# Two chunks of one batch taken out of the casting load: fp32 load, a fold on GpSimd and VectorE, and a quadrant first stage

## The chip, the cores and the metric

The kernel runs on one core of a Trainium2 chip. The metric is the device time of one execution in microseconds. It is told as a median over runs, and a profiled execution has a time of its own beside the span of its trace.

## The reference

Two layers follow each other. The first filters x (8 batches, 3072 rows, 256 columns) along the rows in the frequency domain: `irfft(rfft(x) * (filt_r + i filt_i))`, column by column. The second takes the result as 24576 tokens of 256 and computes `max(h @ w1, h @ w2) @ w_out`, with 1024 hidden columns. Input and output are fp32.

## The kernel before

The row index of a batch is split as p * 32 + m, with 96 values of p and 32 of m. The filter is then a chain of small stages: a transform over p (first stage), a transform over m with the filter's product (second), the way back (third and fourth). The feed-forward layer works on 64 tiles of 384 tokens, eight to a batch. It is written as max(a, b) = max(a - b, 0) + b, so one hidden product with Wd = w1 - w2 (`moe_h`, L656, evicted as a relu), and an output product with Wo and M = w2 w_out (`moe_o`, L718 and L720).

All instruction streams are written out by hand. The main loop (L989 to L1018) goes through 64 steps for each batch. A step issues one `moe_h`, then what `mid` holds for it, then three to eight matmuls of `moe_o` for the tile before, and last what `plan` has put at that step. `now` and `later(n, ...)` put a call n steps on. So the stages of batch b + 1 are strewn between the tiles of batch b, and each engine takes its instructions strictly in the order in which they were issued. In `plan(0, 10, ...)` the first number is the batch, the second the step.

Until the main loop, batch 0 is brought through all its stages at once. Batch 1 has its own first stage, and all later batches another:

- **Batch 1** is loaded by `load_x` (L120) on GpSimd's DMA queue, which casts fp32 to bf16 on the way; one call takes two of the batch's eight chunks (chunk c holds m = 4c to 4c + 3). The calls for chunks 2 and 3, then `load_wo` (Wo), then a `prep_wd`, then the calls for chunks 4 and 5 and for 6 and 7 follow each other there (L880 to L884), and GpSimd's further `prep_wd` and `cast_w2` come behind them. `f1` (L359) does the first stage for two values of m: one matmul of the 96-column table C1 with 96 x 512 of x, evicted by ScalarE (even c) or VectorE (odd c) into `at`; after every second one SyncE stores the result to a scratch tensor `ad` in DRAM. `f1(1, 0)` to `f1(1, 3)` stand ahead of the loop, `f1(1, 4)` to `f1(1, 15)` at steps 5 to 12, and `f1_read` (L376) at step 13 reads it back transposed into `bt`, in three DMAs.
- **Batches 2 to 7** are loaded by `load_xf` (L127) in fp32, on SyncE's DMA queue, into one of three buffers XF[(8b + c) % 3], as two halves of 48 partitions each (g = 0, 1). In the first use of each buffer two more DMAs of 16 partitions (L134) fill the rows between. `fold` (L137) on GpSimd makes sum and difference of the two halves of p (L140, L141), in bf16. `s1` (L383) then needs only half-size transforms, which stand on quadrants of TensorE: for batch 2 four matmuls 64 x 64 x 512 (L397), for the others eight with 32 columns (L403). ScalarE evicts both of its PSUM tiles (L407), and `s1_store` writes them to `ad`.

In batch 0's steps, `plan_f2` puts `load_xf(2, c)` at steps 8, 8, 10, 12, 17, 20, 24, 28 and `fold(2, c)` at 10, 13, 16, 20, 24, 27, 30, 33. `visit` (L578) at step 25 is the first that reads batch 1's `bt` (`s2`, L435). PSUM has six banks for all of these tiles, in rotation, and two for the output.

SyncE's DMAs share eight semaphores in turn: in the built program each of its DMAs waits for the completion of the one eight places before it, besides waiting for its data.

The lines of the prediction: L125 is the issue of `load_x`, L130 and L134 of `load_xf`, L330 of Wo, L374 of `f1`'s store, L380 of `f1_read`, L341 and L348 are `prep_t` and `prep_m` (they build M), L366 is `f1`'s matmul and L369 its eviction on VectorE, L629 and L635 belong to `s4` (fourth stage), L793 to `t2`, L441 and L518 are products with the filter on VectorE, L281 is table arithmetic at the start.

Of the kernel before, what the change touches and what calls it, by code (L numbers as in the profile page):

```python
# [27 lines left out]
def kernel(  # L28
# [98 lines left out]
    def load_xf(b, c):  # L127
        src = x[b].rearrange("(h p m) d -> p h m d", h=2, m=NM)
        for g in range(2):
            nc.sync.dma_start(out=XF[(8 * b + c) % 3][64 * g:64 * g + 48],  # L130
                              in_=src[:, :, 4 * c + 2 * g:4 * c + 2 * g + 2, :])
            if b == 2 and c < 3:

                nc.sync.dma_start(out=XF[(8 * b + c) % 3][64 * g + 48:64 * g + 64],  # L134
                                  in_=src[0:16, :, 4 * c + 2 * g:4 * c + 2 * g + 2, :])

    def fold(b, c):  # L137
        t_ = x_tile(b, c).rearrange("p (s m) d -> p s m d", s=2)
        f = XF[(8 * b + c) % 3]
        G.tensor_tensor(t_[:, 0], f[:, 0], f[:, 1], OP.add)  # L140
        G.tensor_tensor(t_[:, 1], f[:, 0], f[:, 1], OP.subtract)  # L141
        xb[b, c] = t_
# [240 lines left out]
    def s1(b, c):  # L383
# [10 lines left out]
        bk.run(0.22)  # L394
        if b == 2:
            for g, r in ((0, 0), (1, 1), (0, 1), (1, 0)):
# [8 lines left out]
        for g in range(2):  # L405
            m0 = 4 * (c % 2) + 2 * g
            S.activation(at[:, m0:m0 + 2], pa[g], AF.Copy)  # L407
            bk.evict("S", 0.48, ks[g])
        if c % 2 == 1:
            later(52 - now[0][1] if c == 7 and b == 3 else 2 if c == 7 and b == 2 else 5 if c == 5 and b == 2 else 3, s1_store, b, c, at)  # L410

    def s1_store(b, c, at):
        for r in range(2):
            nc.sync.dma_start(out=ad[b][48 * r:48 * r + 48, 4 * c - 4:4 * c + 4], in_=at[64 * r:64 * r + 48])

# [466 lines left out]
    prep_wd(0, G)  # L882
    for c in (4, 6):
        load_x(1, c, 2)  # L884
    for q in range(1, 4):
# [13 lines left out]
    t2(0, (V, S))  # L899
    f1(1, 1, V)  # L900
    spin(1, I128, U[:, 0:8].rearrange("p u c -> p (u c)"))
    s4(0)
# [146 lines left out]
```

## Time and profile before

| What | us |
| --- | --- |
| median of 3 runs | 490.0 (489.99 to 490.71) |
| the profiled execution, its own time | 489.1 |
| span of its trace | 487.3 |
| PE (matmul) busy | 475.9, 98% of the span |
| DVE (VectorE) busy | 362.4, 74% |
| ACT (ScalarE) busy | 307.4, 63% |
| POOL (GpSimd) busy | 296.0, 61% |

The 1.8 us between the execution's own time and its span lie around the trace. A busy share is a mean over stages with different limits, and matmuls are pipelined, so the chain of work that ended last says more than the share. In that chain each piece has its start, its length, its engine and its line; where a piece of the same kind is longer at one place than at another, the engine lost time there. The timeline has for each row the start, the length, and in brackets the idle time ahead of it with what ended it. "SPq" is SyncE's DMA queue: a row tells when the issue began, not when the data landed.

### The profile page before, as it was taken

The numbers are of one execution on the slowest core, as the hardware profiler recorded it, in microseconds if no ns is written. First come the engines' busy times: TensorE is split into PE (matmuls) and PEld (weight loads), VectorE is DVE, ScalarE is ACT, GpSimd is POOL, SyncE is SP. The second block draws the span as 40 slices with busy tenths as digits, with TensorE's granted clock in tenths as the row PEclk, the third lists the DMA queues.
The fourth block names the chain that finished last, engine by engine and source line by source line (L and its number), as shares of the span: only waits on it lengthen the run. The fifth ranks groups of instructions, "written<-read, shape, count | busy, mean of one in ns | idle before, by whom it ended". The sixth has DMA issues, their size and how long they took to land.

```text
span 487.3 us, 15411 instructions
## 1 busy us (share of the span) xinstructions
PE 475.9 (98%) x6204; PEld 342.3 (70%) x6207; DVE 362.4 (74%) x589; ACT 307.4 (63%) x645; POOL 296.0 (61%) x378
## 2 busy tenths in 40 slices
PE   8689999999999999999999999999999999999996
PEld 4457777776677676776677676776777776777775
DVE  7886789987876878677786778777885878775542
ACT  5877488667764778468764677467774556354442
POOL 8695868559980698739874698738951266111110
PEclk9979999999999999999999999999999999999999
DMA  8999999898766889789876897789556523541112
GB/s 124 172 247 228 263 255 270 272 254 241 216 180 193 214 270 282 222 237 265 234 187 199 237 261 222 221 245 248 169 165 213 175 88 107 174 156 66 66 66 86
DMA packets 87816, 97.37 MB, mean 200 GB/s; under 512 B 9281, under 2 KB 67938, under 8 KB 87650
## 3 DMA queue, kind: packets, MB, share of 16 engines
q1 hardware_dynamic: 79010, 79.30, 57.7%
q0 software_dynamic: 8592, 17.01, 13.8%
q8 instruction: 48, 0.79, 0.7%
q14 instruction: 22, 0.18, 0.1%
q10 hardware_dynamic: 144, 0.09, 0.1%
HBM read 53.87 MB, written 47.19 MB: 207 GB/s over the span
## 4 chain that ended last, share of the span: by engine, by line
PE 93%; DVE 2%; DMA 2%; POOL 1%; issue 1%; ACT 0%; DVEq 0%; POOLq 0%
PE po L720 36%; PE ph L656 34%; PE po L718 9%; PE pc L612 3%; PE pa L403 2%; PE pz L547 2%; PE px L493 2%; DMA xb<-in_x_dram 2%; DVE pq L441 1%; DVE F L164 1%; PE pr L793 1%; POOL xb L125 1%; PE pz L459 1%; PE pa L366 1%; PE py L629 1%
## 5 line engine op out<-in xcount | busy, mean ns | idle before, releaser
L720 PE MATMUL po<-Wo,gt 128*128 128x256 bf16 x1528 | 263.1, 273 | 0.0
L661 ACT ACTIVATE gt<-ph 128x384 bf16<-128x384 f32 x347 | 165.9, 502 | 141.6 <-PE ph L656 136.8
L720 PEld LDWEIGHTS <-gt 128*128 128x128 bf16 x1528 | 144.2, 98 | 66.4 <-issue 12.4
L658 DVE TENSOR_SCALAR gt<-ph 128x384 bf16<-128x384 f32 x165 | 90.6, 552 | 46.2 <-PE ph L656 44.5
L656 PEld LDWEIGHTS <-Wd 128*128 128x128 bf16 x1024 | 99.0, 98 | 14.1 <-DVE pf L507 0.7
L668 POOL DMA_DIRECT2D out_dram<-ot x86 | 48.8, 568 | 98.1 <-DVE ot L731 87.8
L140 POOL TENSOR_TENSOR xb<-XF 128x512 bf16<-128x512 f32 x48 | 61.1, 1274 | 51.3 <-DMA XF<-in_x_dram 44.4
L503 DVE TENSOR_TENSOR pf<-px,F 128x1024 f32<-128x1024 f32 x60 | 71.1, 1218 | 18.7 <-PE px L493 7.0
L731 DVE TENSOR_SCALAR ot<-po 128x512 f32<-128x512 f32 x83 | 57.0, 686 | 18.8 <-PE po L720 18.2
L141 POOL TENSOR_TENSOR xb<-XF 128x512 bf16<-128x512 f32 x48 | 61.0, 1272 | 0.0
L407 ACT ACTIVATE at<-pa 128x512 bf16<-128x512 f32 x96 | 50.0, 603 | 4.0 <-PE pa L403 3.1
L533 POOL TENSOR_TENSOR ri<-pf 128x256 bf16<-128x256 f32 x60 | 43.8, 730 | 14.3 <-DVE pf L503 14.1
L534 POOL TENSOR_TENSOR ri<-pf 128x256 bf16<-128x256 f32 x60 | 43.6, 727 | 0.0
L556 ACT ACTIVATE zt<-pz 128x512 bf16<-128x512 f32 x60 | 31.3, 600 | 9.2 <-PE pz L547 9.2
L617 ACT ACTIVATE ce<-pc 128x384 f32<-128x384 f32 x56 | 23.7, 490 | 3.5 <-PE pc L612 2.1
L441 DVE TENSOR_TENSOR pq<-px,F 128x1024 bf16<-128x1024 f32 x19 | 22.1, 1219 | 2.6 <-PE px L435 2.3
L403 PE MATMUL pa<-xb,CT 64*32 64x512 bf16 x320 | 16.2, 381 | 0.0
L612 PEld LDWEIGHTS <-zr 48*128 48x128 bf16 x896 | 12.6, 93 | 4.4 <-issue 3.6
L612 PE MATMUL pc<-G,zr 48*128 48x48 bf16 x896 | 14.8, 180 | 0.0
L493 PE MATMUL px<-bt,U 64*32 64x256 bf16 x432 | 14.4, 272 | 0.0
L514 DVE TENSOR_TENSOR pf<-px,F 128x1024 f32<-128x1024 f32 x6 | 7.4, 1226 | 5.0 <-POOL ri L534 4.3
L804 PE MATMUL pd<-W 128*128 128x512 bf16 x26 | 9.5, 496 | 1.5 <-DVE zero L186 1.5
(415 smaller groups left out, 735.5 us busy)
## 6 DMA issues: line engine op xcount, KB each, us to landing
XF<-in_x_dram SPq DMA_DIRECT2D x96, 192.0 KB
out_dram<-ot SPq DMA_DIRECT2D x101, 128.0 KB
out_dram<-ot POOLq DMA_DIRECT2D x90, 128.0 KB, 3.5
ad<-at SPq DMA_DIRECT2D x56, 192.0 KB
zd<-zt SPq DMA_DIRECT2D x42, 256.0 KB
bt<-ad SPq DMA_DIRECT2D x72, 128.0 KB
zr<-zd SPq DMA_DIRECT2D x24, 192.0 KB
zr<-zd SPq DMA_DIRECT2D x28, 96.0 KB
```

What stands on the lines that cost most here:

```text
L140: G.tensor_tensor(t_[:, 0], f[:, 0], f[:, 1], OP.add)
L141: G.tensor_tensor(t_[:, 1], f[:, 0], f[:, 1], OP.subtract)
L407: S.activation(at[:, m0:m0 + 2], pa[g], AF.Copy)
L503: V.tensor_tensor(t_, px[s].rearrange("p (o k) d -> p o k d", o=1).to_broadcast([128, 2, 2, D]), F[:, :, 2 * n, s].rearrange("p c (o d) -> ...
L533: G.tensor_tensor(ri[:, s, 0], t_[:, 0, 0], t_[:, 1, 1], OP.subtract)
L656: TE.matmul(ph, Wd[:, dc, 128 * j:128 * j + 128], y_[:, dc], start=(dc == 0), stop=(dc == 1))
L658: V.tensor_scalar(gt[tt][:, j], ph, 0.0, None, OP.max)
L661: S.activation(gt[tt][:, j], ph, AF.Relu)
L668: E.dma_start(out=dst, in_=src)
L718: TE.matmul(p_, y_[:, n, blk], M[:, n], start=(e == 0), stop=(e == 9))
L720: TE.matmul(p_, g_[:, n - 2, blk], Wo[:, n - 2], start=(e == 0), stop=(e == 9))
L731: V.tensor_scalar(ot[tt // 2][:, e - 1:e + 1], po[q // 2 % 2], SCALE, None, OP.mult)
```

## The change

Chunks 6 and 7 of batch 1 no longer come through `load_x`. They are loaded by `load_xf` in fp32, issued ahead of the loop right behind the store of `f1(1, 1)`. They take buffers 2 and 0 of XF, whose first use (with L134) they now are; the third first use is `load_xf(2, 0)`, which keeps buffer 1. So `load_xf(2, 1)` now has to wait for the fold of chunk 6, and `load_xf(2, 2)` for that of chunk 7. `fold(1, 6)` stands on GpSimd at step 6, `fold(1, 7)` on VectorE at step 10. Both first stages stand together at step 13, in `mid`, so ahead of that step's `moe_o`, in the four-matmul form that batch 2 had. ScalarE evicts the one PSUM tile of each and VectorE the other. The store follows two steps later, with rows in the order that `f1_read` reads, and `f1_read` moves from step 13 to 16. `f1(1, 12)` to `f1(1, 15)` fall away at steps 11 and 12; the other first-stage calls keep their steps. The `load_xf` calls of batch 2 keep theirs too.

```diff
-            if b == 2 and c < 3:
+            if 14 <= 8 * b + c < 17:
...
-    def fold(b, c):
+    def fold(b, c, engine=G):
...
-        G.tensor_tensor(t_[:, 0], f[:, 0], f[:, 1], OP.add)
-        G.tensor_tensor(t_[:, 1], f[:, 0], f[:, 1], OP.subtract)
+        engine.tensor_tensor(t_[:, 0], f[:, 0], f[:, 1], OP.add)
+        engine.tensor_tensor(t_[:, 1], f[:, 0], f[:, 1], OP.subtract)
...
-        if b == 2:
+        if b <= 2:
             for g, r in ((0, 0), (1, 1), (0, 1), (1, 0)):
                 TE.matmul(pa[g][64 * r:64 * r + 64], CT[64 * g:64 * g + 64, r], xb[b, c][64 * g:64 * g + 64, r],
...
-            S.activation(at[:, m0:m0 + 2], pa[g], AF.Copy)
+            if b == 1 and g == 1:
+                V.tensor_copy(at[:, m0:m0 + 2], pa[g])
+            else:
+                S.activation(at[:, m0:m0 + 2], pa[g], AF.Copy)
...
     def s1_store(b, c, at):
         for r in range(2):
-            nc.sync.dma_start(out=ad[b][48 * r:48 * r + 48, 4 * c - 4:4 * c + 4], in_=at[64 * r:64 * r + 48])
+            if b == 1:
+                dst = ad[b].rearrange("(u s r) m d -> s u r m d", s=2, r=2)[r][:, :, 4 * c - 4:4 * c + 4]
+            else:
+                dst = ad[b][48 * r:48 * r + 48, 4 * c - 4:4 * c + 4]
+            nc.sync.dma_start(out=dst, in_=at[64 * r:64 * r + 48])
...
-    for c in (4, 6):
-        load_x(1, c, 2)
+    load_x(1, 4, 2)
...
     t2(0, (V, S))
     f1(1, 1, V)
+    for c in (6, 7):
+        load_xf(1, c)
...
-        for c, n in zip(range(4, 16), steps):
+        for c, n in zip(range(4, 12), steps):
...
-    plan_f1(0, 1, (5, 6, 7, 7, 9, 9, 10, 10, 11, 11, 12, 12), 13)
+    plan(0, 6, fold, 1, 6)
+    plan(0, 10, fold, 1, 7, V)
+    mid[0, 13] = [(s1, (1, 6)), (s1, (1, 7))]
+    plan_f1(0, 1, (5, 6, 7, 7, 9, 9, 10, 10), 16)
```

The `later` call of `s1` gives batch 1's store two steps instead of three; no other number in it differs.

More of the change, by code (lines that the diff above doesn't have):

```diff
@@ L406, in s1 @@
             m0 = 4 * (c % 2) + 2 * g
[L407 removed]
+            if b == 1 and g == 1:
+                V.tensor_copy(at[:, m0:m0 + 2], pa[g])
+            else:
+                S.activation(at[:, m0:m0 + 2], pa[g], AF.Copy)
             bk.evict("S", 0.48, ks[g])
         if c % 2 == 1:
[L410 removed]
+            later(52 - now[0][1] if c == 7 and b == 3 else 2 if c == 7 and b == 2 else 5 if c == 5 and b == 2 else 2 if b == 1 else 3, s1_store, b, c, at)
     def s1_store(b, c, at):
         for r in range(2):
[L414 removed]
+            if b == 1:
[3 more added lines that the diff above has]
+            nc.sync.dma_start(out=dst, in_=at[64 * r:64 * r + 48])
     def s1_read(b, v):
```

## The prediction

> **What bounds the kernel now.** I read the page first: span, busy shares, the DMA slices, the chain that ended last.
>
> ```profile
> span 487.3 us, 15411 instructions
> ...
> PE 475.9 (98%) x6204; PEld 342.3 (70%) x6207; DVE 362.4 (74%) x589; ACT 307.4 (63%) x645; POOL 296.0 (61%) x378
> ...
> DMA  8999999898766889789876897789556523541112
> ...
> PE 93%; DVE 2%; DMA 2%; POOL 1%; issue 1%; ACT 0%; DVEq 0%; POOLq 0%
> ```
>
> The reader is to see that TensorE sets the end, with 93% of the chain, and that the DMA engines are eight to nine tenths busy in the slices (12.2 us each) of the first 120 us, where the change lies. Next the waits of TensorE from 34 to 80 us, the stretch that the change touches:
>
> ```profile
> PE pr L793 <- DVE zT L780: 0.3, 1, 0.3
> ```
>
> One wait of 0.3 us, and no other. So every microsecond of matmul that goes away here comes off the end, every new wait of TensorE is added to it, and there is hardly an old wait to win. Then the chain in order of time, for the price of each piece:
>
> ```profile
> 41.32 0.55 PE pt L341 x8
> ...
> 43.53 0.45 PE pt L341 x8
> ...
> 49.20 0.43 PE pa L366 x2
> ...
> 50.40 0.43 PE pa L366 x2
> ...
> 51.17 0.33 PE ph L656 x2
> ...
> 54.44 0.44 PE po L720 x4
> ...
> 61.45 0.34 PE px L435 x8
> 61.79 0.22 PE pa L397 x4
> 62.01 0.54 PE po L720 x4
> ...
> 64.87 0.22 PE px L435 x8
> ```
>
> Columns: start, length, what. The pair at 49.20 stands at step 11, that at 50.40 at step 12, the ph at 51.17 is step 13, the px at 61.45 is step 25, the first use of batch 1's bt. L435 and L397 are matmuls on quadrants. Coming from the full array eight px take 0.34, behind other quadrant work 0.22: the way in costs 0.12. Four po take 0.44 in general, but 0.54 behind quadrants: the way out costs 0.10.
>
> **The change, part by part.**
>
> *First stage on TensorE.* Four f1 matmuls go: two pairs at 0.43, so -0.86. Two s1 calls come, each four L397 matmuls at 0.22, so +0.44, and as they stand between full-array matmuls they pay 0.12 in and 0.10 out: +0.66. Net **-0.20**.
>
> *One casting load less on GpSimd.*
>
> ```profile
> 33.28 0.93 POOL L330 DMA_DIRECT2D Wo<-in_moe_w_out_dram  x1
> ...
> 35.42 1.06 POOL L125 DMA_DIRECT2D xb<-in_x_dram  x2
> ...
> 42.39 0.58 POOL L232 COPY CT<-C 48x96 bf16<-48x96 bf16 x2
> ...
> 50.17 1.27 POOL L140 TENSOR_TENSOR xb<-XF 128x512 bf16<-128x512 f32 x1 [7.20 <-DMA XF<-in_x_dram]
> 51.40 1.27 POOL L141 TENSOR_TENSOR xb<-XF 128x512 bf16<-128x512 f32 x1
> ```
>
> Half of the row at 35.42 goes, 0.53, and what follows on GpSimd comes that much earlier. Of this TensorE feels prep_t at 41.32, which waits for w2b: 0.55 there, 0.45 for the same work at 43.53. So **-0.10**. GpSimd is free from 42.97 to 50.17; fold(1, 6), 1.27 + 1.27, fits if chunk 6 lands by 47.6. Without that cover it would push fold(2, 0) back, and through it SyncE (below).
>
> *The fold and the evictions on VectorE.* No row shows VectorE folding from SBUF to bf16. The nearest:
>
> ```profile
> L369 DVE CAST at<-pa 96x512 bf16<-96x512 f32 x8 | 5.5, 683 | 3.1 <-PE pa L366 3.0
> ...
> L518 DVE TENSOR_TENSOR pf<-px,F 128x512 f32<-128x512 f32 x6 | 4.1, 681 | 0.0
> ...
> L281 DVE TENSOR_TENSOR ua<-ua,ru 128x768 f32<-128x768 f32 x2 | 1.9, 958 | 0.1
> ```
>
> L281 reads SBUF twice: 958 ns for 768 columns, scaled to 512 some 640; L518 takes 681 for 512. So 1.28 to 1.36 for the two halves, and I take 1.36. Two L369 evictions go (-1.37), two s1 evictions of the same 512 columns come (+1.37), so VectorE has 1.36 more between steps 10 and 16. Where it stands:
>
> ```profile
> 47.39 0.69 DVE L369 CAST at<-pa 96x512 bf16<-96x512 f32 x1 [2.06 <-PE pa L366]
> 48.59 0.69 DVE L369 CAST at<-pa 96x512 bf16<-96x512 f32 x1 [0.51 <-PE pa L366]
> ...
> 51.48 0.54 DVE L635 TENSOR_SCALAR y__1241<-py 128x384 bf16<-128x384 f32 x1
> ```
>
> The fold starts behind the first of these, 48.08, and ends at 49.44. Behind it wait f1(1, 11)'s eviction (to 50.13), step 12's relu and s4's half (by L635 0.54 each, to 51.2), then the two s1 evictions (0.69 each, to 52.6). TensorE wants f1(1, 11)'s bank again six tiles later, in s1(1, 6): at 51.17 + 0.33 - 0.86 + 0.12 = 50.76, so 0.6 after it is free; the relu's bank goes to s1(1, 7) at 50.98, 0.3 after; s4's is wanted at step 14, later still. **0**, with half a microsecond to spare; each microsecond by which VectorE is later than this beyond 0.3 to 0.6 stops TensorE as long.
>
> *SyncE's queue.* This is where the change may cost.
>
> ```profile
> 36.80 7.21 SPq L374 DMA_DIRECT2D ad<-at  x4
> 44.06 0.56 SPq L130 DMA_DIRECT2D XF<-in_x_dram  x1
> 44.67 1.11 SPq L134 DMA_DIRECT2D XF<-in_x_dram  x1
> ...
> 46.35 0.43 SPq L134 DMA_DIRECT2D XF<-in_x_dram  x1
> ...
> 51.80 0.82 SPq L374 DMA_DIRECT2D ad<-at  x2
> 52.72 0.92 SPq L130 DMA_DIRECT2D XF<-in_x_dram  x2
> 56.12 2.18 SPq L380 DMA_DIRECT2D bt<-ad  x3
> ```
>
> Eight new issues come behind the store at 36.80. By the issues from 44.06 on (0.43 to 1.11 each) they last some 4.5 us, to 41.7; in before SyncE sat in that stretch waiting for data of the three stores behind, and the last of these ends at 44.01. The next eight DMAs each wait for one of the new loads to complete: load_xf(2, 0), whose four issues ran from 44.06 to 46.78, waits for loads issued at about 39.4 to 40.8, which is 5 us before. As load_xf(2, 0) itself landed at 50.17, 3.4 us after its last issue, I take it as unmoved. Chunk 6 is then down by about 43, chunk 7 by 45.5, ahead of both folds. load_xf(2, 1) and (2, 2) lose four issues of L134 and gain waits for folds that end at about 45.6 and 49.4; they went at 46.82 and 49.76.
>
> What moves is the end. load_xf(2, 3), step 12, needs fold(2, 0), which ends at 51.40 + 1.27 = 52.67: it goes at 52.72 to 53.64 as before. In before the last store of batch 1 stood ahead of it (51.80 to 52.62); now it stands behind, at step 15, so at 53.64 to 54.46. From the end of the store's issue to f1_read's start were 56.12 - 52.62 = 3.50; so f1_read comes at 57.96, **1.84 later**. TensorE reads bt at 61.45 - 0.30 = 61.15, 3.19 after that, where it had 5.33. How long the first of the three reads takes isn't in the trace. Bounds:
>
> ```profile
> out_dram<-ot POOLq DMA_DIRECT2D x4, 128.0 KB, 4.9
> ...
> 58.50:59.00 0.50, 0.50 (x9) 0.48 (x8) 0.00 (x0) 0.48 (x1) 0.50 (x2) 1.00 0.91 128
> 59.00:59.50 0.50, 0.50 (x9) 0.40 (x7) 0.10 (x1) 0.01 (x1) 0.49 (x2) 1.00 0.48 105
> ```
>
> From above: GpSimd's output stores in this stretch, 4.9 from issue to landing; a wait of 1.7. From below: at 59.00 the share of the DMA engines (last column but one) falls to 0.48, as if what was issued at 56.12 was through by then, 2.9; no wait. The store to read 3.50 and load_xf(2, 0)'s 3.4 lie nearest, being SyncE's own DMAs in this crowd: 3.4 gives a wait of **+0.20**, and I take it. The second read, wanted 3 us later, has more room. A gain is excluded: nothing waited at 61.45.
>
> *Sum.* -0.20 - 0.10 + 0.20 = **-0.1**: 489.0 for the profiled execution (489.1), and 489.9 beside the median of 490.0.
>
> **The rivals.**
>
> *A, bt is late.* The point is 3.19 us: if f1_read's first DMA takes longer, TensorE stops at step 25 for the rest, nothing behind it can be pulled ahead, and the end moves as much. At 4.9 the wait is 1.7 instead of 0.2: 490.0 - 0.3 + 1.7 = 491.4, slower. Every delay of load_xf(2, 0) adds to it, since load_xf(2, 3) and with it the store hang on fold(2, 0). For it: busy DMA engines. Against it: the lull at 59.00.
>
> *B, VectorE's fold collides with GpSimd.* Price: if each of its two halves has to wait for a GpSimd instruction of 1.27 to end, the fold takes 1.36 + 2.54, f1(1, 11)'s bank comes at 52.67 instead of 50.13, TensorE stops 52.67 - 50.76 = 1.9: 490.0 - 0.3 + 0.2 + 1.9 = 491.8. It decides only if GpSimd folds between 48.1 and 49.4, so if chunk 6 lands after about 45.6. The rows put GpSimd's folds at 43 to 45.6 and from 50.17 on; against it. (The Trainium skill, SBUF — State Buffer, section "Who interferes with whom", has that a VectorE instruction with two SBUF inputs contends with a GpSimd instruction that reads SBUF; no two such rows of this trace lie on each other, so it is open here, and by that rule the time is that of B.)
>
> *C, Wo comes late.*
>
> ```profile
> Wo<-in_moe_w_out_dram POOLq DMA_DIRECT2D x1, 512.0 KB, 9.2
> ...
> DMA to landing us min/median/max: 9.4/10.2/11.0
> ...
> 43.81 0.60 PE L720 MATMUL po<-Wo,gt 128*128 128x256 bf16 x4
> ```
>
> The second row is of the loads of chunks 4, 5 (issued 35.42) and 6, 7 (0.53 later). Wo lands at 33.28 + 9.2 = 42.5 and is used at 43.81. The load of chunks 6 and 7 stood behind it in one queue; now its bytes run beside it. They took 35.95 + 11.0 - 35.42 - 9.4 = 2.1 of transfer. Should all of it come ahead, Wo lands at 44.6, and TensorE, there at 43.7, waits 0.9: 490.8 with the forecast's other terms. Half of it costs nothing. Against it: those 2.1 were run beside load_xf(2, 0), and were no longer than the 2.3 from Wo to chunks 4, 5. (The Trainium skill, DMA: Bandwidth & Descriptors, section "Queues, rings and completion order", lets each DMA engine take turns between its queues packet by packet; by that half the bytes would come ahead, and the sum stays.)
>
> *D, more is won.* The quadrant switches are hidden at step 13 and bt is in time: -0.86 + 0.44 - 0.10 = -0.52, 489.5. For more than 1 us the waits of TensorE hold nothing.
>
> **How the numbers follow.** A measurement tells 0.2%, 0.98 us, from no change. The forecast, bt in time or late by at most 1.2, has 0.54; D 0.12, C 0.05. These lie within 0.2%, less 0.02: same 0.69. A has 0.15, B 0.04, and 0.06 goes to delays on SyncE that I haven't seen: slower 0.25. For faster stay 0.06: the 0.02 and 0.04 for a gain that no row shows. The range goes from below D, 489.2, to A's end, 491.4; B and half of the unseen lie above it. The likeliest case's own range is 489.7 (no wait) to 490.9 (1.2).
>
> **What would show it.** In the chain: the f1 pairs at steps 11 and 12 gone, two pa of 0.22 at step 13 with a longer po behind them. The fold on VectorE 1.3 to 1.4 long, GpSimd's extra fold over before 48. f1_read near 58.0; if TensorE's waits name L435 at step 25, A is right, and its length is A's price. A wait of L720 near 43.7 would be C, of L397 near 51 would be B. I am wrong if load_xf(2, 0) lands much later than 50.2, or if a wait shows beyond 62 us, where I take everything as moved by one constant.

## The result, and the profile after

The changed kernel takes 493.4 us (median of 10 runs, 491.9 to 496.5) beside 490.5 of the kernel before (10 runs on the same chip, 489.4 to 492.4). The ratio is 1.0061 (95%: 1.0036 to 1.0087), so it is slower, by 1.8 to 4.3 us. 489.9 was forecast, with 491.4 as the upper end. Below, one of e1's eleven runs (498.05 us), over 1.5% above its fastest, is left out.

The profiled execution took 493.3. The page of the changed kernel, the rows that answer to those of before:

```profile
span 491.3 us, 15434 instructions
...
PE 476.4 (97%) x6211; PEld 341.6 (70%) x6211; DVE 362.7 (74%) x591; ACT 307.3 (63%) x645; POOL 299.8 (61%) x379
...
PE 93%; DMA 3%; ACT 2%; POOL 1%; issue 1%; DVE 0%; SPq 0%; POOLq 0%
```

TensorE is as busy as before. In the chain DMA has 3% instead of 2%: two transfers of 3.24 and 2.94 us are new between 59 and 65 us. ScalarE's 2% stands for the most part in the setup, where the chain of before ran over VectorE. TensorE's waits from 34 to 80 us (behind the arrow what it waited for; then us in total, times, longest) say where:

```profile
PE px L442 <- DMA bt<-ad: 1.6, 1, 1.6
PE pt L779 <- issue: 0.8, 1, 0.8
PE pr L800 <- DVE zT L787: 0.3, 1, 0.3
PE pa L397 <- ACT at L410: 0.3, 1, 0.3
```

From L410 on a line has a number that is 7 higher than in the kernel before: L442 is the px of step 25, L663 `moe_h`, L725 and L727 `moe_o`, L800 `t2`, L341 `prep_t` as before, L410 ScalarE's eviction of a first-stage quad (the four matmuls of one chunk). Two waits of the main loop are new: bt at step 25 and an eviction at step 13 (that of `pt` lies in the setup). The chain of the changed kernel in order of time:

```profile
36.73 0.63 PE pr L800 x8
...
42.94 0.45 PE pt L341 x8
...
51.48 0.34 PE py L636 x8
51.82 0.33 PE ph L663 x2
52.15 0.54 PE pa L397 x4
52.69 0.04 issue
52.72 0.61 ACT at L410
53.33 0.04 issue
53.37 0.41 PE pa L397 x3
...
54.32 0.33 PE ph L663 x2
...
58.88 0.15 SPq L421
59.03 0.05 issue
59.08 3.24 DMA ad<-at
...
62.46 2.94 DMA bt<-ad
65.40 0.04 issue
65.44 0.41 PE px L442 x8
```

The first row is the first `t2`, where nothing of the change has run yet. In the chain of before it is this row:

```profile
35.11 0.63 PE pr L793 x8
```

So this execution was 1.62 us later before the change began. The other programs below lie 0.1 to 1.2 behind that row as well (2.8 and 3.0 in two that zero buffers first), and before's profiled execution is itself 1.4 below the median of its runs. I therefore subtract this offset, piece by piece:

| Piece of the path | before | after | difference |
| --- | --- | --- | --- |
| first `t2` to `moe_h` of step 13 | 35.11 to 51.17 | 36.73 to 51.82 | -0.97 |
| step 13 (ph to the next ph) | 0.77 | 2.50 | +1.73 |
| step 14 to the first px of step 25, its wait for bt | | | +1.67 |
| from there to the end | | | +0.18 |
| sum | | | +2.6 |

The last two rows are read from the starts of the 95 output evictions on VectorE: against before they are +2.38 late up to 60 us, +4.06 from 68 us on, +4.24 at the end. The sum agrees with the 2.9 between the medians.

Where bt's lateness starts stands in SyncE's queue, changed kernel:

```profile
38.42 0.33 SPq L374 DMA_DIRECT2D ad<-at  x1
38.80 0.73 SPq L130 DMA_DIRECT2D XF<-in_x_dram  x1
...
42.19 0.46 SPq L130 DMA_DIRECT2D XF<-in_x_dram  x1
45.70 0.31 SPq L134 DMA_DIRECT2D XF<-in_x_dram  x1
46.93 1.47 SPq L374 DMA_DIRECT2D ad<-at  x3
48.45 0.42 SPq L130 DMA_DIRECT2D XF<-in_x_dram  x1
...
52.81 5.11 SPq L130 DMA_DIRECT2D XF<-in_x_dram  x4
58.03 1.82 SPq L421 DMA_DIRECT2D ad<-at  x2
62.46 1.56 SPq L380 DMA_DIRECT2D bt<-ad  x3
```

The seventh new issue is at 42.19, the eighth at 45.70. Each DMA waits for the one eight places before it; for the eighth new one that is the store at 38.42, and it took until 45.7. So SyncE stands for 3.0 us. The store at 46.93 has in its turn the first new load, issued at 38.80, eight places before it, and SyncE stands another 0.9 us for that. `load_xf(2, 0)` goes at 48.45 instead of 44.06: 2.77 later without the offset. GpSimd's folds follow it:

```profile
47.94 1.26 POOL L140 TENSOR_TENSOR xb<-XF 128x512 bf16<-128x512 f32 x1 [3.48 <-DMA XF<-in_x_dram]
49.17 1.26 POOL L141 TENSOR_TENSOR xb<-XF 128x512 bf16<-128x512 f32 x1
54.62 1.26 POOL L140 TENSOR_TENSOR xb<-XF 128x512 bf16<-128x512 f32 x1 [4.19 <-DMA XF<-in_x_dram]
```

The third row is `fold(2, 0)`, at 50.17 in before (2.83 later without the offset). `load_xf(2, 3)` waits for it and holds up what stands behind it in SyncE's queue: batch 1's last store (58.03) and the read (62.46). VectorE's fold of chunk 7 ran into GpSimd's second half:

```profile
49.51 1.47 DVE L140 TENSOR_TENSOR xb<-XF 128x512 bf16<-128x512 f32 x1
50.90 0.68 DVE L141 TENSOR_TENSOR xb<-XF 128x512 bf16<-128x512 f32 x1
```

### The profile page after: what moved, and what is told of

The parts are those of the page before. It is cut to its first block, busy times and chain, and to the rows that moved or that the text cites. A ratio compares the mean times of both kernels' runs of the same rounds, so it can differ in the third digit from the quotient of the medians.

```text
span 491.3 us, 15434 instructions
## 1 busy us (share of the span) xinstructions
PE 476.4 (97%) x6211; PEld 341.6 (70%) x6211; DVE 362.7 (74%) x591; ACT 307.3 (63%) x645; POOL 299.8 (61%) x379
## 4 chain that ended last, share of the span: by engine, by line
PE 93%; DMA 3%; ACT 2%; POOL 1%; issue 1%; DVE 0%; SPq 0%; POOLq 0%
PE po L727 35%; PE ph L663 34%; PE po L725 9%; PE pc L619 3%; PE pa L403 2%; PE pz L554 2%; PE px L500 2%; DMA xb<-in_x_dram 2%; PE pt L779 1%; POOL xb L125 1%; PE pz L466 1%; PE pr L800 1%; DMA ad<-at 1%; PE pt L773 1%; DMA bt<-ad 1%
## 5 line engine op out<-in xcount | busy, mean ns | idle before, releaser
L727 PE MATMUL po<-Wo,gt 128*128 128x256 bf16 x1528 | 263.1, 273 | 0.0
L727 PEld LDWEIGHTS <-gt 128*128 128x128 bf16 x1528 | 144.2, 98 | 66.4 <-issue 12.4
L663 PEld LDWEIGHTS <-Wd 128*128 128x128 bf16 x1024 | 99.1, 98 | 13.8 <-DVE pf L514 0.7
L140 POOL TENSOR_TENSOR xb<-XF 128x512 bf16<-128x512 f32 x49 | 62.3, 1271 | 57.6 <-DMA XF<-in_x_dram 50.4
L141 POOL TENSOR_TENSOR xb<-XF 128x512 bf16<-128x512 f32 x49 | 62.2, 1269 | 0.0
L410 ACT ACTIVATE at<-pa 128x512 bf16<-128x512 f32 x98 | 51.2, 604 | 6.2 <-PE pa L403 3.3
L540 POOL TENSOR_TENSOR ri<-pf 128x256 bf16<-128x256 f32 x60 | 43.6, 727 | 10.5 <-DVE pf L510 10.3
L500 PE MATMUL px<-bt,UN 64*32 64x256 bf16 x144 | 10.3, 269 | 0.0
```

The lines of the kernel that those rows point to most:

```text
L140: engine.tensor_tensor(t_[:, 0], f[:, 0], f[:, 1], OP.add)
L141: engine.tensor_tensor(t_[:, 1], f[:, 0], f[:, 1], OP.subtract)
L540: G.tensor_tensor(ri[:, s, 0], t_[:, 0, 0], t_[:, 1, 1], OP.subtract)
L663: TE.matmul(ph, Wd[:, dc, 128 * j:128 * j + 128], y_[:, dc], start=(dc == 0), stop=(dc == 1))
L727: TE.matmul(p_, g_[:, n - 2, blk], Wo[:, n - 2], start=(e == 0), stop=(e == 9))
```

## The experiments

Three theories: **Q**, the number and order of SyncE's DMAs make bt late; **T**, the bytes of the new loads, beside the others, make transfers slow; **V**, the pair of first stages at step 13, with VectorE's evictions, stops TensorE. All times are medians, beside the kernel before on the same chip.

| Run | us | before | ratio (95%) | larger new waits of TensorE in the profile |
| --- | --- | --- | --- | --- |
| e8 new loads alone | 492.06 | 490.86 | 1.0033 (1.0017 to 1.0049) | bt 1.1 |
| e13 the same, 32 KB | 491.03 | 490.76 | 1.0011 (0.9993 to 1.003) | bt 0.8 |
| e1 read ahead of a load | 492.97 | 490.11 | 1.0059 (1.0033 to 1.0084) | scratch `zd` of batch 1, 2.1; L410 0.3 |
| e9 order, quads apart | 491.05 | 490.14 | 1.0024 (1.0001 to 1.0046) | bt 0.8 |
| e12 order, quads together | 491.92 | 490.42 | 1.0034 (1.0013 to 1.0055) | Wo 2.4, casting load 0.4, L410 0.3 |
| e3 quads apart, 12 and 14 | 493.93 | 490.11 | 1.008 (1.0054 to 1.0106) | bt 4.0 |
| e4 e1 and e3 | 492.62 | 490.11 | 1.0059 (1.0034 to 1.0084) | fold 1.1 |
| e5 both folds on GpSimd | 494.57 | 490.86 | 1.007 (1.0043 to 1.0097) | bt 2.6, fold 0.4 |
| e2 loads in the setup | 494.42 | 490.11 | 1.009 (1.0069 to 1.0111) | chunks 2, 3: 2.1; Wd 0.7 |
| e6 fills in the setup | 495.94 | 490.86 | 1.0098 (1.0071 to 1.0126) | Wo 3.3, casting load 0.9, bt 0.6 |
| e7 the same, order mended | 495.85 | 490.86 | 1.0094 (1.0058 to 1.013) | Wo 3.1, Wd 1.1 |
| e10 loads on GpSimd's queue | 494.66 | 490.14 | 1.0088 (1.006 to 1.0117) | an eviction behind chunk 7's fold 2.3, bt 1.0 |
| e11 the same, order mended | 495.03 | 490.14 | 1.0095 (1.0063 to 1.0127) | the same 1.7, bt 0.3 |
| e14 change, loads of 32 KB | 493.28 | 490.76 | 1.0055 (1.0036 to 1.0075) | L414 (eviction) 0.3 |
| e15 the same, quads apart | 493.33 | 490.76 | 1.005 (1.0031 to 1.007) | bt 0.9 |
| e16 no fills, order mended | 490.76 | 490.76 | 1.0015 (0.9997 to 1.0032) | bt 0.8, Wo 0.6 |
| e17 e16, two loads later | 492.17 | 490.15 | 1.0041 (1.0023 to 1.0059) | bt 1.1 |
| e18 e17, zeroing on ScalarE | 491.68 | 490.15 | 1.0029 (1.0016 to 1.0043) | bt 0.8 |

A profile is one execution: the waits tell mechanisms, the ratios, which go over the single runs and are not the quotients of the medians, what they cost.

The waits leave out one loss. From 36 to 120 us TensorE's granted clock is 1.00 in the profiles of before and of the changed kernel. In e2, e3, e5 and e12 it falls to 0.50 for 3.4 to 6.8 us at the end of a long wait (2.1, 4.0, 2.6 and 2.4), and in e1 near 102 us, so these profiles lose more than their waits: from 60 to 68 us e3's output evictions fall back 6.5 us, with a wait of 4.0. In e6, e7 and e10, with waits of 3.3, 3.1 and 2.3, it stays at 1.00; what decides isn't shown. Over all its runs the changed kernel's mean clock is 0.992, as in before (0.9915 to 0.9922 beside the experiments), so this is not what makes it slower. In e3, e5, e7, e11, e14 and e15 the mean is 0.988 to 0.990; by estimate 1 to 2 us of their times are due to that (0.002 to 0.004 of 490).

### The new loads alone

In the kernel before, the condition of L134 is set as in the change and the eight issues are added, nothing else (e8).

```diff
-            if b == 2 and c < 3:
+            if 14 <= 8 * b + c < 17:
...
     f1(1, 1, V)
+    for c in (6, 7):
+        load_xf(1, c)
```

> The kernel before, to which only the eight new issues of the fp32 loads of chunks 6 and 7 are added, at their place behind the c = 1 store; nobody reads what they bring, and batch 1 is done as before (so 1 MB is loaded in vain). Theory Q: SyncE stops at the eighth for 3 us as in the changed kernel, fold(2, 0) begins 3 to 4 us late, and f1_read behind it by about 2 us; as the stores of batch 1 stand ahead of the fold's wait here, the read is just in time or late by less than 1 us: ratio 1.000 to 1.003. Theory V (the quadrant stage, its evictions and the fold on VectorE cost, the loads don't): no change at all on SyncE beyond 1 us.

The loads alone cost 1.2 us, and bt is late by 1.1 without any of the compute of the change. Then the same eight issues with one partition each (e13). As they don't fill the rows between, `load_xf(2, 1)` and `load_xf(2, 2)` keep their L134 here, four issues more than in e8:

```diff
+            n = 1 if b == 1 else 48
-            nc.sync.dma_start(out=XF[(8 * b + c) % 3][64 * g:64 * g + 48],
-                              in_=src[:, :, 4 * c + 2 * g:4 * c + 2 * g + 2, :])
+            nc.sync.dma_start(out=XF[(8 * b + c) % 3][64 * g:64 * g + n],
+                              in_=src[0:n, :, 4 * c + 2 * g:4 * c + 2 * g + 2, :])
-            if b == 2 and c < 3:
+            if 8 * b + c in (14, 15, 16, 17, 18):
...
+                n = 1 if b == 1 else 16
...
```

> The kernel before with eight further issues on SyncE at the place where the changed kernel has its new loads, but each moves one partition of 4 KB instead of 48 of 192 KB or 16 of 64 KB (32 KB in all instead of 1024 KB), and nothing reads them. With the full loads the same run gave 1.0033 (1.0017 to 1.0049). If the bytes are the cause (T), the eighth issue does not stop or stops under 1 us, the first load of batch 2 is issued within 1 us of where before has it (44.1), its fold begins near 50 to 51, TensorE does not wait at step 25, and the time is that of before, ratio under 1.0015. If the number and place of the issues are the cause (Q), SyncE stops at the eighth as with the full loads, the fold begins near 55 and the ratio stays near 1.003.

SyncE's queue in that run (L131 and L136 are the two issues of `load_xf`, L376 the store of `f1`):

```profile
41.35 0.56 SPq L131 DMA_DIRECT2D XF<-in_x_dram  x1
45.03 0.56 SPq L136 DMA_DIRECT2D XF<-in_x_dram  x1
45.71 1.36 SPq L376 DMA_DIRECT2D ad<-at  x3
47.12 0.44 SPq L131 DMA_DIRECT2D XF<-in_x_dram  x1
```

The stop at the eighth issue is there with 32 KB as with 1 MB, and `load_xf(2, 0)` comes 2.7 late as in the changed kernel (47.12 - 44.06, less 0.38 of offset). So Q is right about the stop: it is the count, and the store eight places before. Bytes are no condition of it. T is right about a part of what follows: the 0.9 us ahead of the store at 46.93 are gone (45.71 comes 0.1 after the eighth issue), the median lies 1.0 lower than with the full loads, though the intervals of the two ratios touch, and Wo landed in 8.7 us here and in 10.7 there.

### The order on SyncE

e1 lets the read go ahead of `load_xf(2, 3)`:

```diff
-            (8, 8, 10, 12, 17, 20, 24, 28), (10, 13, 16, 20, 24, 27, 30, 33))
+            (8, 8, 10, 17, 17, 20, 24, 28), (10, 13, 16, 20, 24, 27, 30, 33))
```

> load_xf(2, 3) goes from step 12 to step 17, behind f1_read, so that the store of batch 1 and the read no longer stand behind the wait for fold(2, 0). Theory Q (the place in SyncE's queue costs: the new loads are slow, load_xf(2, 0) and its fold come late, and store and read stand behind them): the store goes some 3 us earlier against the work around it, TensorE's wait of 1.6 us at the first px of step 25 goes away, the stretch from the first t2 in the chain to the end of that px falls from 29.1 us to about 27.5 (26.7 in the kernel before), and the time falls by 1.5 to 2 us against the changed kernel, to a ratio of about 1.002 to 1.003. Theory T (the added traffic makes the store and the read themselves slow): the wait stays above 1 us. Theory V (the pair of first stages at step 13 and VectorE cost): the wait at step 13 stays, 1.1 us more than worked out, and the time changes by less than 0.5 us.

bt is in time, but nothing is won. Eight DMAs (four loads of batch 2) are pushed back together, the first store to batch 1's scratch `zd` behind them is issued at 75.3 instead of 66.0 in before, and TensorE waits near 100 us:

```profile
PE pc L619 <- DMA zr<-zd: 2.1, 2, 1.3
```

e9 puts the last store ahead of `load_xf(2, 3)`, and the quads apart (store still at step 15):

```diff
-            later(... else 2 if b == 1 else 3, s1_store, b, c, at)
+            later(... else 1 if b == 1 else 3, s1_store, b, c, at)
...
-    mid[0, 13] = [(s1, (1, 6)), (s1, (1, 7))]
-    plan_f1(0, 1, (5, 6, 7, 7, 9, 9, 10, 10), 16)
+    mid[0, 13] = [(s1, (1, 6))]
+    mid[0, 14] = [(s1, (1, 7))]
+    plan_f1(0, 1, (5, 6, 7, 7, 9, 9, 10, 10), 17)
...
-            (8, 8, 10, 12, 17, 20, 24, 28), (10, 13, 16, 20, 24, 27, 30, 33))
+            (8, 8, 10, 16, 17, 20, 24, 28), (10, 13, 16, 20, 24, 27, 30, 33))
```

> The changed kernel with its loads where they are, but s1(1, 6) at step 13 and s1(1, 7) at step 14, the store of batch 1 ahead of load_xf(2, 3) on SyncE and f1_read right behind that load (step 17). Theory Q (order on SyncE): the read no longer hangs on fold(2, 0) through the store, the wait at step 25 falls from 1.6 to 6 us to below 0.5, nothing later is pushed back, ratio 1.000 to 1.003. Theory T (the new loads run beside Wo and chunks 4 and 5, and whatever is transferred between 37 and 60 us is late by a varying amount): single executions still show waits for Wo, chunk 6 or bt, and the median stays at 1.004 or more.

That takes away some two thirds of the loss: 0.9 us of it are left. e12 does the order alone (steps 17 and 16 as above, the pair left at step 13):

> The changed kernel with only the order on SyncE mended: load_xf(2, 3) at step 16, f1_read at step 17, so that batch 1's store at step 15 goes ahead of both, on the same steps as in the run with order and two quads apart (ratio 1.0024). Both first stages stay together at step 13. If the place of the store in SyncE's queue is what the change costs (Q), this is the same as that run, 490.7 to 491.4 us beside a before of 490.1: the store's issue comes near 55, the read near 61, and TensorE waits for bt at step 25 at most 0.9 us, where the changed kernel waited 1.6. If it is the pair at step 13 with VectorE's evictions (V), the piece from step 13 to step 14 stays 2.5 us long where before had 0.77 (0.66 more was worked out), and the time is 0.5 to 1.1 us above that run: 491.6 to 492.3. If it is the traffic of the new loads beside the casting loads (T), order changes nothing and the time stays at that of the changed kernel, 493 us, with a wait moved to another place.

1.5 us are left, so V has a part too, as step 13 lasted 2.50 here again; the intervals of e9 and e12 overlap widely. Its profiled execution took 494.8, far above the run's median, and another wait stands in it. Behind the wait four matmuls of `moe_o` take 1.01 us at half the clock, where they take 0.44 in general:

```profile
PE po L727 <- DMA Wo<-in_moe_w_out_dram: 2.4, 1, 2.4
```

```profile
47.07 1.01 PE po L727 x4
```

Wo landed 13.1 us after its issue, where before had 9.2 and the changed kernel's profile 10.5. Up to step 11 the order of all queues is that of the changed kernel, as it is in e3 and e4, where Wo landed in 9.1. So the landing varies from execution to execution, and may be what makes some of the changed kernel's runs 3 us longer than others; it is shown for this one only.

### The pair at step 13

e3 stands the quads at steps 12 and 14, with the store at 15; e4 is e3 and e1 together:

```diff
-    mid[0, 13] = [(s1, (1, 6)), (s1, (1, 7))]
+    mid[0, 12] = [(s1, (1, 6))]
+    mid[0, 14] = [(s1, (1, 7))]
...
```

> The two first stages of batch 1 stand apart, s1(1, 6) at step 12 and s1(1, 7) at step 14, store one step behind it at 15 as before; nothing else differs from the changed kernel. Theory V: TensorE's wait between the two calls (some 1.1 us at step 13) goes away, and the time falls by about 1 us. Theory Q: the wait goes away, but as the moment of the read is set by SyncE's queue, TensorE only comes earlier to the px of step 25 and waits there 2.6 us instead of 1.6; the time doesn't change by more than 0.5 us.

> Both edits at once: first stages at steps 12 and 14, load_xf(2, 3) behind the read. Theory Q with V's wait: both waits go, the stretch from the first t2 to the end of step 25's px comes to about 26.5 us, as in the kernel before less 0.2, and the time is that of the kernel before within 0.2% (ratio 0.998 to 1.001). Theory T: the wait at step 25 stays over 1 us.

In both the stop at step 13 is gone (in e3, from the first `t2` to step 16, TensorE is 0.78 better than in the changed kernel), but it is no gain: in e3 TensorE waits 4.0 for bt, in e4 1.1 for the fold of chunk 6, which step 12 is too early for. e5 has `fold(1, 7)` on GpSimd (`plan(0, 10, fold, 1, 7)`):

> One part undone: chunk 7 is folded by GpSimd at step 10 instead of VectorE. In the changed kernel VectorE's first half took 1.47 us beside a fold of GpSimd, the second 0.68. Theory V: with no fold on VectorE its evictions ahead of step 13 come 2 us earlier, and the wait at step 13 falls from 1.1 to below 0.5 us; the time falls by 0.5 to 1 us. Theory Q: fold(2, 0) still waits for its load (GpSimd has over 4 us free ahead of it, the fold takes 2.5), the wait at step 25 stays at 1.5 to 4 us or grows by what step 13 gives back, and the time stays within 0.5 us.

It waits 0.4 for that fold, and 2.6 for bt. What stops TensorE at step 13 is in the built programs, in the PSUM banks that they give to the tiles. From f1(1, 11)'s tile on:

| | f1 | ph | ph | py | py | ph | first quad | second quad |
| --- | --- | --- | --- | --- | --- | --- | --- | --- |
| changed kernel, e12, e14 | 4 | 7 | 2 | 6 | 5 | 3 | 7, 6 | 3, 7 |
| e5 | 4 | 7 | 2 | 6 | 5 | 3 | 4, 7 | 2, 6 |
| e16 | 4 | 7 | 2 | 6 | 5 | 3 | 7, 4 | 2, 6 |

The banks don't rotate strictly. In the first row bank 4 is left out, and the second quad takes bank 7, which the first quad has just filled: its second matmul waits for ScalarE's eviction (the row ACT at L410 in the chain; bank 3 is that of the step's own ph, whose eviction ends before). In e16 neither quad takes a bank of the other, and the same pair on the same step runs through (TensorE of e16; L661 is `moe_h`, L395 the quads):

```profile
51.98 0.49 PE L661 MATMUL ph<-y__1059,Wd 128*128 128x384 bf16 x2
52.40 0.63 PE L395 MATMUL pa<-xb,CT 64*64 64x512 bf16 x8
...
53.41 0.49 PE L661 MATMUL ph<-y__1059,Wd 128*128 128x384 bf16 x2
```

From ph to ph it is 1.43, that is 0.77 + 0.66: what was worked out, to the hundredth. The banks of the first row cost 1.07.

### The loads in another place

e2 issues the eight loads in the setup, behind the w1 and w2 loads (the two lines of `load_xf(1, c)` moved up to behind `fix_f()`). e6 issues the six fills of 16 partitions there, from batch 0's rows, and e7 adds e9's order to it:

```diff
-            if 14 <= 8 * b + c < 17:
-                nc.sync.dma_start(out=XF[(8 * b + c) % 3][64 * g + 48:64 * g + 64],
-                                  in_=src[0:16, :, 4 * c + 2 * g:4 * c + 2 * g + 2, :])
+    def fill_xf():
+        src = x[0].rearrange("(h p m) d -> p h m d", h=2, m=NM)
+        for k in range(3):
+            for g in range(2):
+                nc.sync.dma_start(out=XF[k][64 * g + 48:64 * g + 64], in_=src[0:16, :, 2 * g:2 * g + 2, :])
...
     fix_f()
+    fill_xf()
```

> The fp32 loads of chunks 6 and 7 are issued some 11 us earlier, on SyncE right behind the loads of w1 and w2 in the setup; all else as in the changed kernel. Theory Q: nothing on SyncE waits for them from step 0 on, load_xf(2, 0) goes at the same distance behind the c = 7 store as in the kernel before, fold(2, 0) is over 2.5 to 3 us earlier against the work around it, the wait of 1.6 us at step 25 goes away, and the time falls by about 1.5 us, if the setup isn't slowed by the loads (they run beside w1, w2 and chunks 0 and 1). Theory T: the same bytes have moved by then, the read is as slow as before and the wait stays. Theory V: no change in the wait at step 13 beyond 0.3 us.

> The six small DMAs of 16 partitions (L134), which fill the rows between the halves of the three fp32 buffers at their first use, are issued in the setup behind the loads of w1 and w2, from other rows of x; the fp32 loads of chunks 6 and 7 are then four issues instead of eight. Else as the changed kernel. Theory Q, now named by its place: the eighth new issue stops SyncE for 3 us until the c = 1 store is complete, and all behind it is that much late. Here that place is reached only by load_xf(2, 0), with two issues instead of four: fold(2, 0) begins 3 to 4 us earlier against the work around it, the read likewise, the wait at step 25 goes away, and the time falls by about 1.7 us to a ratio of 1.002 to 1.003; the 1.1 us at step 13 stay. Theory T (the loads are slow for the traffic, whatever stands in SyncE's queue): fold(2, 0) stays within 1 us of the changed kernel's, and the wait stays.

> The small fills in the setup, and besides s1(1, 6) at step 13 and s1(1, 7) at step 14, the store of batch 1 ahead of load_xf(2, 3) on SyncE and f1_read behind it (step 17). Theory Q with the wait of the pair: both waits go, nothing later is pushed back (unlike with load_xf(2, 3) behind the read), the stretch from the first t2 to the end of step 25's px is 26.5 us as against 26.7 in the kernel before, and the time is that of the kernel before less 0 to 0.3 us (ratio 0.999 to 1.001). Theory T: a wait of over 1 us at step 25, ratio 1.004 or more.

All three are worse. bt is in time in e2 and e7, but the casting loads of GpSimd's queue are late: Wo lands in 14.1, 15.9 and 15.6 us (9.2 in before), and TensorE waits 2 to 3 us for it or for chunks 2 and 3. That is rival C's transfer; that it is the bytes that delay it (T) is argued, not shown. e10 puts the four large loads on GpSimd's queue, behind `table_ct`; e11 adds e9's order:

```diff
...
-            nc.sync.dma_start(out=XF[(8 * b + c) % 3][64 * g:64 * g + 48],
+            (G if b == 1 else nc.sync).dma_start(out=XF[(8 * b + c) % 3][64 * g:64 * g + 48],
...
```

> The four large fp32 loads of chunks 6 and 7 are issued on GpSimd's queue, behind its last setup work, so behind Wo and chunks 4 and 5 as the casting load was; only their four small fills stay on SyncE. Steps as in the changed kernel. Theory T: Wo and chunks 4 and 5 land as in the kernel before (9 us after their issue); SyncE isn't stopped for 3 us; load_xf(2, 0) goes within 1.5 us of its distance in the kernel before; what is left is a wait for chunk 7's landing at step 10 to 13, some 1 to 2 us, and the read behind it: ratio 1.001 to 1.004, with a smaller spread than the changed kernel's 5 us. Theory Q alone (SyncE's place, not the traffic): the same for SyncE, but no change for Wo and chunks 4 and 5.

> Both edits: the large loads on GpSimd's queue behind its setup work, the first stages at steps 13 and 14, the store ahead of load_xf(2, 3), the read behind it. Theory T and Q together: no wait at step 25, at most 1 us for chunk 7's landing, ratio 0.999 to 1.002, and a spread as small as that of the kernel before (2 to 3 us). If the quadrant stage's gain of 0.2 us comes through, this is where it can be seen.

Wo is in time again (10.0 and 10.6), but chunk 7 lands at 51.5 in e10, too late for step 13, with VectorE's evictions queued behind its fold. No place was found at which these loads cost nothing.

### Few bytes in the changed kernel

e14 is the changed kernel with the loads of e13 and VectorE zeroing two buffers at the start, so that it leaves chunks 6 and 7 of batch 1 out; e15 has the quads at 13 and 14 besides.

> The changed kernel with the same small loads in place of the new ones, so chunks 6 and 7 of batch 1 are not brought in; the folds and first stages work on buffers 0 and 2 as two memsets on VectorE at the very start left them (about 1 us each, where it waits for GpSimd). If the bytes are the cause (T): no wait at step 25 and none for Wo; from the first t2 to step 13 0.97 us less than before, at step 13 1.07 more than was worked out (0.66), so in all 0 to +0.3 us against before, 490.0 to 490.9. If the number and place of the issues are the cause (Q): bt still late by 1 to 2 us, 491.5 to 493. If the pair at step 13 and VectorE (V) make most of the changed kernel's 2.9 us, it stays above 492 with no transfer late.

> As the run with small loads in the changed kernel, with the two first stages apart, at steps 13 and 14, the store at step 15 as there. Here no load is late, so this is the price of the pair alone. If the pair waits for VectorE's evictions or PSUM tiles (V), this is 0.5 to 1.1 us faster than with the pair together, and TensorE has no wait of 0.3 for an L410 eviction at step 13: under T 489.3 to 490.2, below the kernel before. If it is the load alone that matters (Q or T without V), the two differ by under 0.3 us.

Both miss what T expected, but they don't speak clearly: their first `t2` comes 3.0 and 2.8 late, with waits for the filter's products ahead of it. Behind these waits the granted clock is 0.72 and 0.78 from 36 to 42 us: the first `t2` took 1.06 and 0.95 instead of 0.62. From there on they lose 1.4 and 1.6. In e14 step 13 lasts 2.50 again, Wo landed in 8.3, and TensorE doesn't wait for bt; in e15 it waits 0.9. That the late start has to do with the zeroing isn't shown; e16 zeroes three buffers and is 1.2 late.

### No fills

e16 is e12 without L134; VectorE zeroes the three buffers once instead.

```diff
-            if 14 <= 8 * b + c < 17:
-                nc.sync.dma_start(out=XF[(8 * b + c) % 3][64 * g + 48:64 * g + 64],
-                                  in_=src[0:16, :, 4 * c + 2 * g:4 * c + 2 * g + 2, :])
...
     V.memset(zero, 0.0)
+    for k in (0, 2, 1):
+        V.memset(XF[k].rearrange("p s m d -> p (s m d)"), 0.0)
```

> The changed kernel in the mended order (load_xf(2, 3) at step 16, f1_read at 17, pair at 13: that run gave 1.0034, 1.0013 to 1.0055), with none of the six issues of 16 partitions: the three buffers are zeroed once by VectorE at the very start instead (three memsets of some 1 us). So there are four new issues on SyncE instead of eight, and 768 KB instead of 1024 KB beside the casting loads; load_xf(2, 0) is one of two issues less. If the number of issues is the cause (Q), SyncE no longer stops at the eighth, load_xf(2, 0) goes within 1 us of before, bt has over 1 us to spare, and the time is 489.8 to 490.6, no slower than before. If it is the bytes (T), a quarter less of them: Wo still lands at 10 to 13 us in some runs, 490.8 to 492. If the memsets hold up VectorE's tables in the setup, everything from the first t2 on is later by that, up to 2 us.

The median is that of before. With four issues fewer SyncE never comes to the eighth, and the banks came out well. What is left in the profile is bt, late by 0.8 still, and Wo by 0.6. The two folds collided again, the other way round (VectorE's two halves, then GpSimd's second half):

```profile
49.83 0.68 DVE L136 TENSOR_TENSOR xb<-XF 128x512 bf16<-128x512 f32 x1
50.43 0.68 DVE L137 TENSOR_TENSOR xb<-XF 128x512 bf16<-128x512 f32 x1
```

```profile
49.59 2.65 POOL L137 TENSOR_TENSOR xb<-XF 128x512 bf16<-128x512 f32 x1
```

`load_xf(2, 1)` stood for that fold on SyncE, with both stores behind it. e17 moves `load_xf(2, 1)` and `(2, 2)` behind the stores; e18 has ScalarE zero two of the buffers besides:

```diff
-            (8, 8, 10, 16, 17, 20, 24, 28), (10, 13, 16, 20, 24, 27, 30, 33))
+            (8, 13, 16, 16, 17, 20, 24, 28), (10, 13, 16, 20, 24, 27, 30, 33))
```

> The run without the 16-partition fills, with load_xf(2, 1) at step 13 and load_xf(2, 2) at step 16 (10 and 12... before: 8 and 10), so that the store of chunks 4 and 5 and then batch 1's last store stand ahead of them in SyncE's queue. There load_xf(2, 1) stood 7.05 us for the fold of chunk 6, and the two stores behind it came at 53.2 and 55.1, the read at 61.0, and bt 0.8 late. If order is what is left (Q): the last store comes near 54.2, the read near 60.1, TensorE waits under 0.2 us at step 25, and the median is 0.6 to 0.9 us below that run's: 489.8 to 490.2 where before is 490.8. If traffic is what is left (T), the store's first half still lands 4.9 us after its issue, Wo still comes late in some runs, and the median is within 0.4 us of that run's, 490.4 to 491. If the later folds of batch 2 show (as in the run with the read moved ahead), there is a wait behind 90 us, 1 us or more.

> The same order, with two of the three buffers zeroed by ScalarE behind its first table (four pieces of 512 columns, some 0.5 to 0.6 us each, where it waited 1.8 us for VectorE), and one by VectorE (0.9 us). With all three on VectorE its first table instruction came at 4.55 instead of 2.21, and the first t2 was 1.2 us later than in the profile of before. If that is the price of zeroing, the first t2 comes 0.5 to 1 us earlier than in the other run of this call, and the time is as much less: 489.2 to 489.8 where before is 490.8. If the setup varies by as much from run to run without cause, the two runs are the same within 0.4 us.

Here Q, which had foretold 489.8 to 490.2 and less, fell. The queue did what it should: the read goes at 58.38 and 57.85, by the forecast's own time (57.96). And yet bt is late by 1.1 and 0.8. The chain of e17:

```profile
54.66 3.65 DMA ad<-at
58.38 5.19 DMA bt<-ad
63.61 0.41 PE px L440 x8
```

The first read took 5.19 us, 4.97 in e18, where the changed kernel's took 2.94. (What e18 was to show, a first `t2` 0.5 to 1 us earlier than e17's, came to 0.3: 35.98 against 36.29.) Side by side, from the chain of every run where it shows both transfers:

| Run | store begins | store takes | read takes | store to px |
| --- | --- | --- | --- | --- |
| e17 | 54.66 | 3.65 | 5.19 | 8.95 |
| e13 | 54.81 | 5.18 | 2.68 | 7.92 |
| e8 | 55.74 | 4.68 | 3.33 | 8.20 |
| e9 | 55.92 | 4.78 | 2.58 | 7.54 |
| e16 | 55.99 | 4.92 | 2.84 | 7.89 |
| e11 | 56.94 | 4.75 | 2.85 | 7.67 |
| e10 | 57.71 | 4.95 | 3.33 | 8.38 |
| e15 | 57.87 | 4.35 | 3.10 | 7.64 |
| e5 | 58.08 | 4.15 | 2.87 | 7.21 |
| changed kernel | 59.08 | 3.24 | 2.94 | 6.36 |
| e3 | 59.34 | 4.06 | 2.78 | 7.02 |
| e6 | 60.18 | 5.21 | 2.64 | 8.03 |

From the store to the px it takes 7.0 to 9.0 us, among batch 2's loads; only the changed kernel is through in 6.4. The late store alone doesn't explain that: e3 and e6 store later still. In before the last store was issued by 52.62 and px came 8.8 later, without a wait. In the versions of the change whose TensorE waits for bt the store was issued at 53.3 at the earliest (e18), and 7.0 to 9.0 us behind it bt is late. In e1 and e4 (54.4 and 54.8) it is in time, but there TensorE comes later to the px by other waits. No version is faster than the kernel before.

## Why the prediction was wrong

**"First stage on TensorE" and "One casting load less on GpSimd": right.** Up to step 13 the four f1 matmuls and the wait for w2b were to give -0.86 and -0.10; measured -0.97 (`prep_t` 0.45 instead of 0.55). The pair was to cost 0.66; it does in e16, and in e18 the path to step 16 is 0.23 shorter than in before, where the two steps together say 0.30.

**"The fold and the evictions on VectorE", put at 0: wrong, 1.07.** The step that failed is "TensorE wants f1(1, 11)'s bank again six tiles later". It took a strict rotation of six banks (as the kernel's description above does); the built program gave the second quad the bank of the first, so TensorE waited for an eviction on ScalarE, which this term doesn't hold at all. The fold itself, 1.36, took 2.07 beside GpSimd, which I had ruled out because chunk 6 was to be down by 43, 3.4 after its last issue; it came at 47.9, 6.9 after it (GpSimd waited for it). By itself that collision cost TensorE nothing that a run shows: step 13 is 2.50 in e12 as well, where VectorE's two halves took 0.68 each.

**"SyncE's queue": wrong, and the larger part.** The step that failed is "I take it as unmoved", of `load_xf(2, 0)`: I counted what the DMAs behind the eight new ones wait for, and not that the eighth itself waits for the store ahead of the first. That store was open for 7 us, and `load_xf(2, 0)` came 2.77 later; e13 shows that the count does it. Through fold(2, 0) the last store then began at 59.08, without the offset 57.46, where 54.46 was forecast. Store and read together took 6.36 to the px, 0.54 less than the forecast's 3.50 and 3.4, and TensorE came to the px 1.06 later than forecast, by step 13: 0.20 + 3.00 - 0.54 - 1.06 = 1.60, the wait that was measured. On the path it is +1.67.

"3.4 gives a wait of +0.20" was too low a price as well, but that did not cost here. Eleven other runs took 7.0 to 9.0 instead of 6.9, and with the read on time it takes 4.97 and 5.19 (e18, e17), just above the upper bound of 4.9. There bt is late by 0.8 and 1.1, so without the first error this term would have been about +1, not +0.20.

**Rival A was the result in its mechanism** and got 0.15; its 1.7 was its upper end and was met from another side, a read 2.9 later (without the offset) that took 2.94. B's collision occurred; the Trainium skill's rule (SBUF — State Buffer, "Who interferes with whom": two such instructions exclude each other, and the order decides which waits) agrees with 1.47 against 0.68 on VectorE (changed kernel) and 2.65 against 1.26 on GpSimd (e16). The prediction found no two such rows on each other in the trace of before; there is one pair, in the setup: four products of L270 (two inputs in SBUF) took 1.35 at 7.08 us, beside GpSimd's cast of L178, and 1.16 at 10.76 without it. B's price, through f1(1, 11)'s bank, did not come. Its sign, a wait of L397 near 51, did show (52.7, without the offset 51.1), but it is that of the shared bank. C cost nothing in the profile (Wo landed in 10.5 and was used 0.7 later) and 2.4 in e12's, so it adds to the spread of the changed kernel's runs. That everything beyond 62 us moves by one constant held within 0.18 here, and fell in e1.

**Open.** Why the setup of one execution is up to 1.6 us later than that of another (of the changed kernel's 1.62, 0.83 are in the first load of x, which took 8.60 instead of 7.77); when the granted clock falls behind a wait; which of the transfers in the crowd makes the store and the read long (no run took batch 2's loads away); and, the intervals being what they are, whether e9, e12, e16, e17 and e18 differ among themselves.

## What to carry to other kernels

Moving work from a queue that has its own pace (the casting load) to one that is issued strictly in order costs at the places behind it: before adding n issues, count back as many places as can be outstanding, and ask of every one, the new ones too, which transfer it waits for and how long that is open. A round trip through DRAM that is moved towards its use is to be priced as a whole, store and read, by the longest that the crowd there shows. When a profile loses more than its waits, look at the granted clock behind them. Where tiles share PSUM banks, look at which bank the built program gives to each, rather than count a rotation.

## What the runs showed of the hardware

- The store of 192 KB ahead of the new loads, at 37 to 38.5, stayed open until about 45 whether 1 MB or 32 KB were loaded behind it (45.70 in the changed kernel, 45.03 in e13).
- Wo's 512 KB, from one place in GpSimd's queue, landed in 9.2 us in before. With the 1 MB of new loads on SyncE behind it, it took 9.1 to 13.1 (9.1 in e3 and e4, 10.5 in the changed kernel, 13.1 in e12), and 14.1 to 15.9 where all or a part of the new DMAs were issued in the setup (e2, e6, e7). The Trainium skill (DMA: Bandwidth & Descriptors, "Queues, rings and completion order") has each DMA engine take turns between its queues; the longer landings agree with it, those of e3 and e4 show no delay.
- The same read of bt took 2.58 to 5.19 us (e9, e17), with no change in its size.
- TensorE's granted clock fell to 0.50 for 3.4 us at the end of a wait of 2.4 us (e12, from 46.7 us) and for 6.8 us at one of 4.0 (e3, from 64.6), and not at waits of 3.3 and 3.1 (e6, e7).
